# A longer TensorE warm-up in a cached grouped-query attention kernel

## The chip, the cores and the metric

The kernel runs on one core of one Trainium2 chip. Its time is the device time of one execution in microseconds (us); several executions are taken and their median is compared. The five engines of the core have instruction queues of their own and wait for one another by semaphores: TensorE (PE in the profile; its weight loads are shown apart as PEld), VectorE (DVE), ScalarE (ACT), GpSimd (POOL) and SyncE (SP), which here issues every DMA. SBUF is the on-chip working memory, PSUM the small memory of eight banks into which TensorE writes.

## The reference

Two independent problems, A and B, of the same shape are computed and joined along the last axis. Each is a block of attention with a cache of keys and values: 16 batches of 80 rows of 576 numbers, 32 query heads, 16 heads of keys and values (two query heads share one), 512 cached positions, heads of 128.

```python
B, Sq, D = 16, 80, 576
Hq, Hkv, Sk, Dh = 32, 16, 512, 128
...
q = (lambda x, *d: x.transpose(*d))((x @ wq).reshape(B, Sq, Hq, Dh), 0, 2, 1, 3)
k = jnp.repeat(k_cache, rep, axis=1)
v = jnp.repeat(v_cache, rep, axis=1)
scores = jnp.einsum("bhqd,bhkd->bhqk", q, k) * (Dh ** -0.5)
p = _softmax(scores, axis=-1)
o = jnp.einsum("bhqk,bhkd->bhqd", p, v)
return (lambda x, *d: x.transpose(*d))(o, 0, 2, 1, 3).reshape(B, Sq, Hq * Dh) @ wo
```

## The kernel before

**Units.** The work is cut into 128 units, each one batch and four of the 16 key-value heads, so eight query heads. Eight units that share the four heads are an octet with its own slice of wq; four octets are a half problem (eight batches, 640 rows); there are four half problems. A unit has five steps of 128 query rows against 512 positions: step 0 collects the last 32 rows of each of the four heads (four column tiles of TensorE side by side, line 431), steps 1 to 4 take the first 128 rows of a head each (line 436).

**A step.** TensorE computes scores into PSUM bank 0, 1 or 2 (line 431 or 436). VectorE takes the negated maximum of each row (441), ScalarE the exponential with the row's sum (445), VectorE the reciprocals for the five steps of a unit (449), GpSimd scales the rows (452). Eight steps after its scores, TensorE transposes the step's probabilities against the identity matrix (458), VectorE copies them out of PSUM (464, 466), TensorE multiplies by V (501), and ScalarE copies the output into oT (513).

**Around it.** The projections of the next octet (335, evicted by 342 and 347) and the output projections (546, evicted by 560 and 566) are laid between the steps. Keys come by a transposing DMA into one of five buffers (405), values into one of four (409); wq slices alternate between two buffers (288, 292, 295).

**Order.** A small scheduler written into the kernel gives every operation a due time by hand. Operations are sorted by it; each engine runs its own in that order; what an operation reads and writes is named, and from these names the scheduler makes semaphore waits between different engines. TensorE's operations among themselves need no waits. All loads stand in SP's one queue in order of due time, so a load that waits for its buffer holds up the loads behind it.

**The start.** POOL fills `ones` (201), makes `ident`, the 128x128 identity (204), and zeroes part of wq_sb (208). VectorE fills `warm` with zeros (215). TensorE's first operation is the warm-up, `em_warm`: NWARM = 8 matmuls of `ones` against `warm`, 512 columns wide, into PSUM bank 0 (220), which nobody reads. It waits for `ones` and `warm`. Behind it in TensorE's queue stand, in this order:

- the transpositions of the first x block by block, 5 blocks of 5 (line 259, `em_xtr`), into banks 7, 5, 6, 3, 4, each block copied out by VectorE (263, `em_xev`);
- the first projections, for the first two batches: 8 groups of 5 matmuls 160 columns wide (335, `em_qp`), into banks 3, 4, 7, 5, 6 in turn, copied out by ScalarE and VectorE in turn;
- the scores of the first unit (431) and, between them, the rest of the first octet's projections, 480 columns wide.

SP's queue begins with the load of x (248), six loads of wq (288, 295, 292, twice), three loads of K (405), and then V (409) and K in turn.

Of the kernel before, what the change touches and what calls it, by code (L numbers as in the profile page):

```python
# [7 lines left out]
F32 = mybir.dt.float32  # L8
# [126 lines left out]
def bass_concat_heads__gqa_block_cached__gqa_block_cached__near_ridge_kernel(  # L135
# [10 lines left out]
    _, G, SK, DH = A_k_cache.shape  # L146
# [13 lines left out]
    with ExitStack() as es:  # L160
        block = es.enter_context(nc.Block())
        sb = lambda name, shape, dt: es.enter_context(nc.sbuf_tensor(name, shape, dt))
        ident = sb("ident", [128, 128], BF16)
        ones = sb("ones", [128, 128], BF16)
        warm = sb("warm", [128, 512], BF16)
        xs = sb("xs", [128, NRT, D], BF16)
        xT = sb("xT", [128, 2, 5, NROW], BF16)
        wq_sb = sb("wq_sb", [128, 2, 5, 1024], BF16)
# [13 lines left out]
        ps = es.enter_context(nc.psum_tensor("ps", [128, 8, 512], F32))  # L182
        psb = ps[:].bitcast(BF16)
# [5 lines left out]
        S = _Sched()  # L189
# [7 lines left out]
        def R(res, ver):  # L197
            return (res, ver)
# [18 lines left out]
        def em_warm(e):  # L217
            last = None
            for _ in range(NWARM):
                last = e.matmul(ps[:, 0, :], lhsT=ones[:], rhs=warm[:], start=True, stop=True)  # L220
            return last

        if NWARM:
            S.add("dve", -1000, em_warmset, writes=[R(("warm",), 0)], name="warmset")
            S.add("pe", -990, em_warm, reads=[R(("ones",), 0), R(("warm",), 0)], writes=[R(("ps", 0), ("W",))],
                  name="warm")
        IDENT = R(("ident",), 0)

        def su_time(goct, bl):
# [4 lines left out]
        for ph in range(NPH):  # L234
# [11 lines left out]
            def em_ldx(e, x_ap=x_ap, half=half):  # L246
# [4 lines left out]
                  name="ldx%d" % ph)  # L251
            for blk in range(NRT):
# [9 lines left out]
                def em_xev(e, blk=blk, xsl=xsl, xb=xb):  # L262
# [5 lines left out]
                      name="xtr%d.%d" % (ph, blk))  # L268
                S.add("dve", tbase[blk] + KO["xev"], em_xev, reads=[R(("ps", xb), pv_)],
                      writes=[R(("xT", xsl, blk), ph)], name="xev%d.%d" % (ph, blk))  # L270

        QB = ((0, 6), (6, 2))
        for goct in range(NPH * NOCT):
# [20 lines left out]
            def em_ldwb(e, wq_ap=wq_ap, q=q, wsl=wsl):  # L294
# [3 lines left out]
                  name="ldwa%d" % goct)  # L298
            S.add("sp", t_ld + 0.01, em_ldwb, writes=[R(("wq", wsl, "b"), goct)], dsem="d_wq%d" % wsl,
                  name="ldwb%d" % goct)  # L300
# [3 lines left out]
            for i in range(8):  # L304
                for c in range(2):
# [40 lines left out]
                    def em_qev_dve(e, qsl=qsl, b0=b0, nb=nb, n0=n0, n1=n1, col=col, bank=bank):  # L346
# [6 lines left out]
                          reads=[R(("wq", wsl, "a"), goct), R(("wq", wsl, "a2"), goct), R(("wq", wsl, "b"), goct),  # L353
                                 R(("wqz",), 0)]
                          + [R(("xT", xsl, b_), ph) for b_ in blks],
                          writes=[R(("ps", bank), pv_)], name="qp%d.%d.%d" % (goct, i, c))
                    S.add(ev_eng, t + t_ev, em_qev_act if ev_eng == "act" else em_qev_dve,
                          reads=[R(("ps", bank), pv_)],
                          writes=[R(("qT", qsl, bl, i), goct) for bl in range(b0, b0 + nb)],
                          name="qev%d.%d.%d" % (goct, i, c))  # L360
# [31 lines left out]
        for U in range(NSU):  # L392
# [5 lines left out]
            _, kc_ap, vc_ap, _, _ = probs[prob]  # L398
# [8 lines left out]
            def em_ldv(e, vc_ap=vc_ap, b=b, q=q, vs=vs):  # L407
# [4 lines left out]
                  name="ldk%d" % U)  # L412
            S.add("sp", t_v - 5.0 * (NV - 1) + KO["ldv"], em_ldv, writes=[R(("V", vs), U)], dsem="d_v%d" % vs,
                  name="ldv%d" % U)

            for k in range(5):
# [55 lines left out]
                else:  # L472
# [3 lines left out]
                      writes=[R(("ps", sbk), ("S", T))], name="qk%d" % T)  # L476
                S.add("dve", tq + KO["max"], em_max, reads=[R(("ps", sbk), ("S", T))],
                      writes=[R(("nm", si), T)], name="max%d" % T)
                t4 = time_of(5 * G + 4)
                S.add("act", tq + KO["exp"], em_exp, reads=[R(("ps", sbk), ("S", T)), R(("nm", si), T)],  # L480
                      writes=[R(("P", psl), ("e", T)), R(("rs", ss, col), G)], name="exp%d" % T)
                if col == 4:
                    S.add("dve", t4 - LA + KO["rcp"], em_rcp, reads=[R(("rs", ss, k_), G) for k_ in range(5)],
                          writes=[R(("ri", ss), G)], name="rcp%d" % G)
                S.add("pool", t4 - LA + KO["nrm"] + 0.01 * col, em_nrm,
                      reads=[R(("ri", ss), G), R(("P", psl), ("e", T))],
                      writes=[R(("P", psl), ("n", T))], name="nrm%d" % T)
                S.add("pe", t0, em_tr, reads=[R(("P", psl), ("n", T)), IDENT],
                      writes=[R(("ps", tb), ("T", T))], name="tr%d" % T)
                S.add("dve", t0 + KO["ptev"], em_ptev, reads=[R(("ps", tb), ("T", T))], writes=pt_writes,  # L490
                      name="ptev%d" % T)

                if k >= 1:
# [4 lines left out]
                    def em_pv(e, gl=gl, ob=ob, off=off, vs=vs, pts=pts):  # L498
                        last = None
                        for j in range(4):  # L500
# [6 lines left out]
                          reads=[R(("V", vs), U), R(("pT", pts, gl, "A"), U), R(("pT", pts, gl, "R"), U)],  # L507
                          writes=[R(("ps", ob), ("O", U, pr))], name="pv%d.%d" % (U, gl))
                    if gl % 2 == 1:
                        hb = 8 * q + 4 * pr  # L510

                        def em_oev(e, ob=ob, hb=hb, bl=bl):
# [4 lines left out]
                              writes=[R(("oT", bl, q, pr), ph)], name="oev%d.%d" % (U, pr))  # L517

        NB_ = NRT * NOC
        for ph in range(NPH):  # L520
            prob, half = divmod(ph, NPP)
            for hh in range(2):
                for n in range(NB_):
                    r, c3 = divmod(n, NOC)
# [29 lines left out]
                    else:  # L554
                        ot_reads = [R(("oT", b_, 0, hh), ph) for b_ in bls]
                    S.add("pe", t, em_op, reads=ot_reads + [R(("wo", hh, wc_), prob) for wc_ in range(NWC)],
                          writes=[R(("ps", bank), pv_)], name="op%d.%d.%d" % (ph, hh, n))
                    if hh == 0:
                        def em_ea(e, r=r, c3=c3, bank=bank):
# [3 lines left out]
                              writes=[R(("acc", r, c3), ph)], name="oea%d.%d" % (ph, n))  # L563
                    else:
# [4 lines left out]
                        def em_st(e, r=r, c3=c3, prob=prob, half=half, slot=slot):  # L569
# [6 lines left out]
                              writes=[R(("osb", slot), (ph, n))], name="oeb%d.%d" % (ph, n))  # L576
# [73 lines left out]
```

## Time and profile before

| | us |
|---|---|
| median of 3 runs | 818.07 |
| lowest and highest | 814.95, 818.31 |
| span of the profiled execution | 812.5 |
| TensorE busy in it | 797.9 |
| VectorE, ScalarE, GpSimd busy | 680.2, 643.4, 433.0 |
| warm-up matmuls (line 220), start to end | 1.34 to 4.91 |
| first transposition of x (line 259) | 5.63 |
| first projection (line 335) | 9.02 |
| first scores (line 431) | 14.99 |

The time of a run and the span of the profiled execution are two measurements: the span goes from the first instruction of the program to the last, the time also holds what lies around it. In the timeline a row is a group of like instructions: its start, its length, the engine, the line of the kernel, the operation, the tile written and the tiles read, the shape and the count; in brackets the engine's idle time ahead of it and what ended that. Matmuls overlap in the array, so that the length of one (0.2 to 0.6 us) says little of the pace; the pace is the distance from one start to the next. A row of waits is the waiting group, what it waited for, then the total in us, the times and the longest.

### The profile page before, as it was taken

Reading aid. Unit: us, or ns where it says so; the run is one execution under the profiler, and the core shown is the slowest. Engines: PE = TensorE matmul, PEld = TensorE weight load, DVE = VectorE, ACT = ScalarE, POOL = GpSimd, SP = SyncE. Lnnn points to the kernel's source line nnn. Section 1 sums busy time; section 2 is a strip of 40 time slices with the busy share of each in tenths; the row PEclk is TensorE's granted clock in tenths of the full one; section 3 lists DMA queues with packets and bytes.
Section 4 is the critical chain, followed back from the end, with each engine's and each line's share of the span. In section 5 each row is a group of like instructions: output and inputs, shape, how many; then the busy total and the mean of one; then the engine's idle time right before and its main releaser. Section 6 shows DMA issues by size and latency. Waiting matters only on the chain.

```text
span 812.5 us, 23206 instructions
## 1 busy us (share of the span) xinstructions
PE 797.9 (98%) x8940; PEld 620.6 (76%) x8940; DVE 680.2 (84%) x1617; ACT 643.4 (79%) x1725; POOL 433.0 (53%) x647
## 2 busy tenths in 40 slices
PE   7999999999999999999999999999999999999998
PEld 4677678777777777877777777777777778777778
DVE  3899988888888889888888889888888888988872
ACT  2899888888878778888887887888887788888860
POOL 1466665455555546555555555555465455555650
DMA  9999999999897999979789999999978879977601
GB/s 228 243 245 283 249 235 268 260 254 219 190 214 182 224 231 214 207 162 223 180 199 240 245 219 230 237 259 223 224 200 191 200 195 214 199 187 172 156 29 37
DMA packets 363629, 169.94 MB, mean 209 GB/s; under 512 B 278017, under 2 KB 354305, under 8 KB 363521
## 3 DMA queue, kind: packets, MB, share of 16 engines
q1 hardware_dynamic: 363520, 168.46, 90.9%
q8 instruction: 73, 1.20, 0.6%
q14 instruction: 36, 0.29, 0.1%
HBM read 98.37 MB, written 2.95 MB: 125 GB/s over the span
## 4 chain that ended last, share of the span: by engine, by line
PE 90%; DVE 5%; DMA 3%; SPq 0%; issue 0%; POOL 0%; ACT 0%; POOLq 0%
PE ps L335 20%; PE ps L546 19%; PE ps L458 18%; PE ps L501 16%; PE ps L436 12%; PE ps L431 5%; DVE negmax L441 3%; DVE pT L466 1%; DMA kT<-in_A_k_cache_dram 1%; DMA v_sb<-in_A_v_cache_dram 1%; DMA wq_sb<-in_A_wq_dram 1%; PE ps L259 1%; POOL p_sb L452 0%; SPq L292 0%; DVE rinv L449 0%
## 5 line engine op out<-in xcount | busy, mean ns | idle before, releaser
L452 POOL TENSOR_SCALAR p_sb<-p_sb,rinv 128x512 bf16<-128x512 bf16 x640 | 430.5, 695 | 354.6 <-DVE rinv L449 354.6
L445 ACT ACTIVATE p_sb<-ps,negmax 128x512 bf16<-128x512 f32 x640 | 442.3, 691 | 83.4 <-DVE negmax L441 65.3
L441 DVE TENSOR_REDUCE negmax<-ps 128x1 f32<-128x512 f32 x640 | 434.4, 679 | 4.5 <-PE ps L436 2.9
L466 DVE COPY pT<-ps 128x512 bf16<-128x512 bf16 x512 | 209.3, 409 | 93.3 <-PE ps L458 92.6
L458 PE MATMUL ps<-ident,p_sb 128*128 128x128 bf16 x2560 | 248.5, 220 | 4.6 <-DVE negmax L441 3.5
L501 PE MATMUL ps<-pT,v_sb 128*128 128x160 bf16 x2048 | 225.3, 233 | 2.6 <-DMA v_sb<-in_A_v_cache_dram 1.3
L458 PEld LDWEIGHTS ps<-ident,p_sb 128*128 128x128 bf16 x2560 | 175.4, 98 | 57.2 <-DVE qT L347 21.6
L501 PEld LDWEIGHTS ps<-pT,v_sb 128*128 128x128 bf16 x2048 | 169.0, 98 | 63.9 <-DVE qT L347 3.6
L335 PE MATMUL ps<-xT,wq_sb 128*128 128x480 bf16 (+1 forms) x1280 | 214.4, 300 | 1.6 <-DMA wq_sb<-in_A_wq_dram 0.9
L436 PE MATMUL ps<-kT,qT 128*128 128x512 bf16 x512 | 194.0, 379 | 0.0
L546 PE MATMUL ps<-wo_sb,oT 128*128 128x192 bf16 x1920 | 175.7, 246 | 0.0
L546 PEld LDWEIGHTS ps<-wo_sb,oT 128*128 128x128 bf16 x1920 | 158.6, 98 | 0.0
L335 PEld LDWEIGHTS ps<-xT,wq_sb 128*128 128x128 bf16 x1280 | 107.0, 98 | 45.0 <-DVE qT L347 0.9
L513 ACT CAST oT<-ps 128x320 bf16<-128x320 f32 x256 | 108.9, 425 | 35.2 <-PE ps L501 32.9
L445 ACT ACTIVATION_READ_ACCUMULATOR p_sb<-ps,negmax 128x1 f32 x640 | 128.1, 200 | 0.0
L342 ACT ACTIVATE qT<-ps 128x480 bf16<-128x480 f32 (+1 forms) x128 | 71.8, 561 | 25.6 <-PE ps L335 25.5
L464 DVE COPY pT<-ps 128x512 bf16<-128x512 bf16 x128 | 52.9, 413 | 1.3 <-PE ps L458 1.3
L431 PE MATMUL ps<-kT,qT 128*32 128x512 bf16 x512 | 51.2, 390 | 1.4 <-DMA kT<-in_A_k_cache_dram 1.4
L436 PEld LDWEIGHTS ps<-kT,qT 128*128 128x128 bf16 x512 | 50.1, 98 | 0.7
L347 DVE TENSOR_SCALAR qT<-ps 128x160 bf16<-128x160 f32 (+1 forms) x128 | 41.5, 324 | 3.8 <-PE ps L335 3.7
L566 DVE TENSOR_TENSOR osb<-ps,acc 128x192 bf16<-128x192 f32 x60 | 21.0, 349 | 15.3 <-PE ps L546 12.2
L431 PEld LDWEIGHTS ps<-kT,qT 128*32 128x32 bf16 x512 | 13.1, 92 | 14.9 <-DMA kT<-in_A_k_cache_dram 1.6
(16 smaller groups left out, 77.5 us busy)
## 6 DMA issues: line engine op xcount, KB each, us to landing
v_sb<-in_A_v_cache_dram SPq DMA_DIRECT2D x64, 512.0 KB, 4.5
v_sb<-in_B_v_cache_dram SPq DMA_DIRECT2D x64, 512.0 KB, 4.5
wq_sb<-in_A_wq_dram SPq DMA_DIRECT2D x16, 512.0 KB, 5.5
wq_sb<-in_B_wq_dram SPq DMA_DIRECT2D x16, 512.0 KB, 5.5
wo_sb<-in_A_wo_dram SPq DMA_DIRECT2D x8, 576.0 KB, 5.4
wo_sb<-in_B_wo_dram SPq DMA_DIRECT2D x8, 576.0 KB, 4.8
out_dram<-osb SPq DMA_DIRECT2D x60, 48.0 KB, 2.1
xs<-in_A_x_dram SPq DMA_DIRECT2D x2, 720.0 KB, 5.1
```

What stands on the lines that cost most here:

```text
L335: last = e.matmul(ps[:, bank, 0:n1 - n0], lhsT=wq_sb[:, wsl, ck, i * 128:(i + 1) * 128], rhs=xT[:, xsl, ck, n0:n1], start=(ck == 0), stop= ...
L342: return e.activation(qT[:, qsl, b0:b0 + nb, col:col + 80], ps[:, bank, 0:n1 - n0].rearrange("p (b s) -> p b s", b=nb), AF.Identity, scale ...
L431: last = e.matmul(ps[32 * g4:32 * g4 + 32, sbk, :], lhsT=qT[:, qsl, bl, g4 * 160 + 128:g4 * 160 + 160], rhs=kT[:, ks, :, g4 * 128:(g4 + 1) ...
L436: last = e.matmul(ps[:, sbk, :], lhsT=qT[:, qsl, bl, gl * 160:gl * 160 + 128], rhs=kT[:, ks, :, gl * 128:(gl + 1) * 128], start=True, stop ...
L441: return e.tensor_reduce(negmax[:, si:si + 1], ps[:, sbk, :], axis=AX.X, op=AluOpType.max, negate=True)
L445: return e.activation(p_sb[:, psl, :], ps[:, sbk, :], AF.Exp, bias=negmax[:, si:si + 1], scale=1.0, accum_out=rowsum[:, ss, col:col + 1])
L452: return e.tensor_scalar(p_sb[:, psl, :], p_sb[:, psl, :], rinv[:, ss, col:col + 1], 1.0, op0=AluOpType.mult, op1=AluOpType.mult)
L458: last = e.transpose(psb[:, tb, j * 128:(j + 1) * 128], p_sb[:, psl, j * 128:(j + 1) * 128], ident[:])
L466: return e.tensor_copy(pT[:, pts, gl, :, 0:128], psb[:, tb, 0:512].rearrange("p (j n) -> p j n", j=4))
L501: last = e.matmul(ps[:, ob, off:off + 160], lhsT=v_sb[:, vs, gl, j * 128:(j + 1) * 128], rhs=pT[:, pts, gl, j, :], start=(j == 0), stop=(j ...
L513: return e.copy(oT[:, hb:hb + 4, bl * SQ:(bl + 1) * SQ], ps[:, ob, 0:320].rearrange("p (h s) -> p h s", h=4))
L546: last = e.matmul(ps[:, bank, 0:DC], lhsT=oT[:, h, r * 128:(r + 1) * 128], rhs=wo_sb[:, h, c3 * DC:(c3 + 1) * DC], start=(hi == 0), stop=( ...
```

## The change

`em_warm` goes on behind its eight matmuls with 160 more, none of whose results is read: transpositions of the identity in two 64-row and four 32-row tiles of TensorE's array, matmuls of 480 columns in two row tiles, matmuls of 512 columns in four column tiles, matmuls of 32, 64 and 96 columns over the whole array, groups of four matmuls of 256 columns between these, and at the end 16 transpositions of a 32-bit float copy of the identity (4 of the whole, 12 in 64-row tiles). They write PSUM banks 0 to 5. VectorE gets one more operation, the copy of `ident` into the new tile `identf`, behind its fill of `warm`. The warm-up's waits grow by `ident` and `identf`, and stand ahead of its first matmul, as the warm-up is one operation of the scheduler.

```diff
@@ -163,6 +163,8 @@
         ident = sb("ident", [128, 128], BF16)
         ones = sb("ones", [128, 128], BF16)
         warm = sb("warm", [128, 512], BF16)
+        identf = sb("identf", [128, 128], F32)
+        identw = identf
         xs = sb("xs", [128, NRT, D], BF16)
         xT = sb("xT", [128, 2, 5, NROW], BF16)
         wq_sb = sb("wq_sb", [128, 2, 5, 1024], BF16)
@@ -218,12 +220,48 @@
             last = None
             for _ in range(NWARM):
                 last = e.matmul(ps[:, 0, :], lhsT=ones[:], rhs=warm[:], start=True, stop=True)
+            for blk in range(12):
+                for h in range(2):
+                    r = slice(64 * h, 64 * h + 64)
+                    e.transpose(psb[:, 1 + h, blk * 64:blk * 64 + 64], ident[r, :], ident[r, r])
+            for _ in range(4):
+                e.matmul(ps[:, 0, 0:256], lhsT=ones[:], rhs=warm[:, 0:256], start=True, stop=True)
+            for blk in range(12):
+                for h in range(4):
+                    r = slice(32 * h, 32 * h + 32)
+                    e.transpose(psb[:, 1 + h, blk * 32:blk * 32 + 32], ident[r, :], ident[r, r])
+            for _ in range(4):
+                e.matmul(ps[:, 0, 0:256], lhsT=ones[:], rhs=warm[:, 0:256], start=True, stop=True)
+            for _ in range(4):
+                for h in range(2):
+                    r = slice(64 * h, 64 * h + 64)
+                    e.matmul(ps[:, 1 + h, 0:480], lhsT=ones[r, :], rhs=warm[r, 0:480], start=True, stop=True)
+            for _ in range(4):
+                e.matmul(ps[:, 0, 0:256], lhsT=ones[:], rhs=warm[:, 0:256], start=True, stop=True)
+            for _ in range(4):
+                for h in range(4):
+                    e.matmul(ps[32 * h:32 * h + 32, 1, :], lhsT=ones[:, 0:32], rhs=warm[:, :], start=True,
+                             stop=True, tile_position=(0, 32 * h))
+            for n_ in (32, 64, 96):
+                for _ in range(12):
+                    e.matmul(ps[:, 2, 0:n_], lhsT=ones[:], rhs=warm[:, 0:n_], start=True, stop=True)
+            for blk in range(4):
+                e.transpose(ps[:, 3, 0:128], identw[:], identw[:])
+            for blk in range(6):
+                for h in range(2):
+                    r = slice(64 * h, 64 * h + 64)
+                    last = e.transpose(ps[:, 4 + h, blk * 64:blk * 64 + 64], identw[r, :], identw[r, r])
             return last
 
         if NWARM:
             S.add("dve", -1000, em_warmset, writes=[R(("warm",), 0)], name="warmset")
-            S.add("pe", -990, em_warm, reads=[R(("ones",), 0), R(("warm",), 0)], writes=[R(("ps", 0), ("W",))],
-                  name="warm")
+            def em_identf(e):
+                return e.tensor_copy(identf[:], ident[:])
+
+            S.add("dve", -995, em_identf, reads=[R(("ident",), 0)], writes=[R(("identf",), 0)], name="identf")
+            S.add("pe", -990, em_warm,
+                  reads=[R(("ones",), 0), R(("warm",), 0), R(("ident",), 0), R(("identf",), 0)],
+                  writes=[R(("ps", b_), ("W",)) for b_ in range(6)], name="warm")
         IDENT = R(("ident",), 0)
 
         def su_time(goct, bl):
```

## The prediction

> **What bounds the kernel now.** First the page: one engine fills the span, and the chain that ended last runs on it.
>
> ```profile
> span 812.5 us, 23206 instructions
> PE 797.9 (98%) x8940; PEld 620.6 (76%) x8940; DVE 680.2 (84%) x1617; ACT 643.4 (79%) x1725; POOL 433.0 (53%) x647
> PE 90%; DVE 5%; DMA 3%; SPq 0%; issue 0%; POOL 0%; ACT 0%; POOLq 0%
> ```
>
> TensorE is 98% busy, so whatever is put into its queue ahead of real work is paid in full unless it lies in one of the few holes. The holes stand in the second view, TensorE's timeline of the first 17 us (start, length, instructions, in brackets the idle time before and what ended it).
>
> ```profile
> 1.34 3.57 PE L220 MATMUL ps<-warm,ones 128*128 128x512 bf16 x8 [1.34 <-DVE warm L215]
> 5.63 2.85 PE L259 MATMUL ps<-ident,xs 128*128 128x128 bf16 x25 [0.72 <-DMA xs<-in_A_x_dram]
> 9.02 3.25 PE L335 MATMUL ps<-xT,wq_sb 128*128 128x160 bf16 x40 [0.54 <-DVE xT L263]
> 13.04 0.51 PE L335 MATMUL ps<-xT,wq_sb 128*128 128x160 bf16 x5 [0.77 <-DMA wq_sb<-in_A_wq_dram]
> 14.99 0.40 PE L431 MATMUL ps<-kT,qT 128*32 128x512 bf16 x4 [1.44 <-DMA kT<-in_A_k_cache_dram]
> ```
>
> The warm-up ends at 4.9, just before x lands (5.63). The last hole closes at 14.99 with the first K load; behind it come projections and scores without a break. So 14.99, the first L431, is the mark I follow: whatever delays it delays all behind it.
>
> The third view, TensorE's waits over the whole span, tells what a delay could win back:
>
> ```profile
> PE ps L458 <- DVE negmax L441: 3.5, 8, 0.4
> PE ps L431 <- DMA kT<-in_A_k_cache_dram: 1.4, 1, 1.4
> PE ps L501 <- DMA v_sb<-in_A_v_cache_dram: 1.3, 1, 1.3
> PE ps L501 <- DVE pT L466: 1.2, 1, 1.2
> PE ps L335 <- DMA wq_sb<-in_A_wq_dram: 0.9, 2, 0.8
> ```
>
> Behind 15 us, start-to-start gaps above their usual add up to 1.5 us at 94.3 (V late), 1.4 at 110.4 (the pT row; the V load issued at 105.78 behind that of the next x is the likely late one) and 0.3 at 58.2 (wq): 3.2 us that loads may explain. The others lie at the end (741 to 788 us) and have nothing to do with the start.
>
> **The change, part by part.** *Removed:* nothing. *Added on VectorE:* one 128x128 copy into identf, for which TensorE's whole warm-up now waits. It waits for ident, which POOL ends at 1.37. The nearest rows are the memset of warm (0.27 us) and the 128x640 copy (0.49); I take 0.27: start about 1.44, end 1.71, and with the 0.14 us from warmset's end to the first matmul (1.20 to 1.34) the warm-up starts at 1.85 instead of 1.34 (bounds 1.65 to 2.05). Behind that wait stands all of TensorE's queue. The eight old matmuls then take 8 x 0.427 = 3.41 (starts 0.427 apart in the trace): 5.26. No DMA is added and SP's queue isn't touched.
>
> *Added on TensorE:* 160 matmuls, each with its weight load. Prices are start-to-start times, since durations overlap (a 128x128 transposition lasts 0.22 but four lie 0.056 apart). At full clock the trace has 0.056 at 128 columns, 0.069 at 160, 0.083 at 192, 0.2025 at 480, 0.2157 at 512: 0.416 ns a column and 2.6 ns on top, the line through 160 and 512, which makes 0.109 of 256 columns. Column tiles are in the trace:
>
> ```profile
> 33.94 0.39 PE L458 MATMUL ps<-ident,p_sb 128*128 128x128 bf16 x4
> 34.25 0.40 PE L431 MATMUL ps<-kT,qT 128*32 128x512 bf16 x4
> 34.59 0.40 PE L458 MATMUL ps<-ident,p_sb 128*128 128x128 bf16 x4
> 34.82 0.38 PE L436 MATMUL ps<-kT,qT 128*128 128x512 bf16 x1
> ```
>
> The four column tiles start within 0.011 us of each other: tiles run side by side. But going in costs 0.093 extra (0.149 from the last transposition's start, not 0.056) and coming out 0.107 (0.323, not 0.216). Row tiles, moving operands under 128 columns and fp32 aren't in the trace; they are bounded by neighbours. In us:
>
> - 24 transpositions in two 64-row tiles: 0.028 each if pairs overlap, 0.056 if not; middle 0.042: 1.0 (0.7 to 1.3).
> - 48 in four 32-row tiles: 0.014 to 0.056, middle 0.035: 1.7 (0.7 to 2.7).
> - 12 matmuls of 256 columns: 1.3.
> - 8 of 480 columns in two row tiles: 0.8 overlapped, 1.6 one by one; 1.2.
> - 16 column-tile matmuls, four rounds: 0.216 (no change of tiling between rounds) to 0.416 each; 1.0 (0.9 to 1.7).
> - 36 of 32, 64 and 96 columns: 0.416 ns a column gives 1.0, the 128-column row 2.0; 1.5.
> - 16 fp32 transpositions: 0.056 as bf16 up to 0.427, the dearest spacing in the trace; I take 0.318, a weight load and a matmul one behind the other (0.098 + 0.220), as fp32 is twice the bytes and nothing says that its load overlaps: 5.1 (0.9 to 6.8). The least certain term.
> - Ten changes of tiling at 0.1: 1.0 (0.4 to 2.0).
>
> Sum 13.8 (6.6 to 19.4). [...]
>
> *Clock.* The granted clock reads 1.00 throughout, yet the starts show two speeds: L220 at 0.427 for 512 columns and L259 at 0.107 for 128 are half speed, L335 goes from 0.133 to 0.069 at 9.71 us. So the clock rose 8.4 us after the first matmul, across two holes. With no hole it should rise earlier: between right after the eighth matmul (cost 0) and 9.71 (half of the 4.5 us from 5.26 lost: 2.2). I take 1.1. [...]
>
> The warm-up ends at 5.26 + 13.8 + 1.1 = 20.2 (11.7 to 27.1).
>
> *What is late next.* x has landed long before, so L259 starts at 20.2. Its 25 at full clock take 1.4 instead of 2.7; VectorE's five copies out of PSUM then set the pace (0.533 apart in the trace, first 0.5 after the start). The first projection reuses the bank of the fourth copy, free after about 2.6, the second that of the fifth, so the row of projections counts from 2.8; 40 x 0.069 = 2.8, and the last copy out (0.2 + 0.33) lets L431 start 6.1 us after L259. Before it was 14.99 - 5.63 = 9.4: the clock and the gone waits for wq (0.8) and K (1.4) give 3.3 back. So L431 starts at 26.3: 11.3 us late.
>
> *Won back behind it.* SP's queue issues without a hole from 0.8 to 96 us; it runs late on its own account, not because buffers are full:
>
> ```profile
> 36.05 0.58 SPq L409 DMA_DIRECT2D v_sb<-in_A_v_cache_dram  x1
> ...
> 87.64 0.51 SPq L409 DMA_DIRECT2D v_sb<-in_A_v_cache_dram  x1
> 88.19 7.43 SPq L405 DMA_TRANSPOSE kT<-in_A_k_cache_dram  x1
> ```
>
> The V load at 36.05 reuses a buffer that TensorE freed at about 33.75, 2.3 us earlier. With TensorE 11.3 later that load waits for the buffer, SP stands 9 us, and from there on loads are ahead by those 2.3 relative to TensorE, no more, however long the warm-up. That removes the wait at 94.3 and part of 110.4: 2.0 (bounds 0 to 3.2).
>
> Sum: 11.3 - 2.0 = +9.3 us of span, 812.5 to 821.8. The median shown is 5.6 above the profiled span; I carry that: **827.4**.
>
> **Rivals.** *The block is short:* row tiles overlap wholly and fp32 goes in one pass. For the block B and the clock's loss c the net is B + c - 5.6 (5.26 - 8.9 - 2.0, where 8.9 is 14.99 - 6.1). Within 4.1 us (0.5%, about what a measurement of this kernel tells from no change) it stays if B + c is under 9.7; at 8.0 the time is 812.5 + 2.4 + 5.6 = 820.5. For it: tiles 3 to 4 ns apart in L431. Against it: four kinds of instruction must all lie near their lower bound. This is the case on the other side: not slower. *The clock stays down:* small work doesn't raise it, the block runs at half speed, 13.8 becomes 27.6, net 27.6 - 5.6 = +22 and 1.6 more for L259 and L335 as now: 842. Against it: the rise at 9.71 came after 2.5 us of transpositions and few matmuls. *Faster:* the block hides in the hole before x. There are only 5.63 - 5.26 = 0.4 us; 160 instructions would have to take 2 ns each. Even without any the gain is about 2 us of clock and 2.0 won back. *Unread work is dropped:* the eight old matmuls, as unread, all stand in the trace.
>
> **Numbers.** Forecast 0.73, short block 0.14, clock down or a block at its upper bounds 0.11, faster 0.02. Slower 0.84, same 0.14, faster 0.02. The range, 821 to 834, is B + c from 8.5 to 21.5; below lies half of the short block, above the half-clock case.
>
> **What would show it.** TensorE's timeline: L259 starts near 20 with idle 0; its 25 take about 1.6; no DMA releaser before L431, which starts near 26. VectorE gains one copy before 2 us. The fp32 rows near 0.32 apart. The V wait at 94 (then near 105) is gone, and the period from 130 us on is unchanged. I am wrong if L431 starts before 21, if the rows of the block lie 14 ns apart, or if the time behind 15 us moves by more than 3 us against L431.

## The result and the profile after

| | before | after |
|---|---|---|
| median of 13 runs each (us) | 816.15 | 820.21 |
| lowest and highest | 814.95, 818.45 | 817.32, 823.58 |
| span of the profiled execution | 812.5 | 818.1 |
| first transposition of x | 5.63 | 14.27 |
| first scores | 14.99 | 20.36 |
| span from the first scores to the end | 797.47 | 797.77 |

The ratio is 1.0043 with a 95% interval of 1.0027 to 1.0059: 4.06 us slower by the medians, a loss that is clear of the noise and about half a per cent. Two later sets of the changed kernel gave 1.0046 [1.0026, 1.0067] and 1.006 [1.0042, 1.0079]. The forecast was 827.4, 9.3 above the 818.07 it started from, and its range began at 821: right in sign, more than twice too large.

The page of the changed kernel, in the lines shown of before: span, busy time of the engines, and the shares of the chain of work that ended last.

```profile
span 818.1 us, 23525 instructions
PE 803.8 (98%) x9100; PEld 623.9 (76%) x9100; DVE 682.0 (83%) x1618; ACT 643.4 (79%) x1725; POOL 434.1 (53%) x647
PE 93%; DVE 5%; DMA 1%; POOL 0%; issue 0%; ACT 0%; POOLq 0%
```

TensorE has 160 matmuls more and 5.9 us more busy time, close to the 5.6 us of span. The share of DMA in the chain falls from 3% to 1%: the holes of the start are filled with warm-up.

The timeline of the changed kernel's start (start, length, engine, line, and in brackets the idle time ahead and what ended it):

```profile
1.31 1.80 POOL L210 MEMSET wq_sb<- 64x2048 bf16 x1
1.40 1.79 DVE L259 CAST identf<-ident 128x128 f32<-128x128 bf16 x1 [0.21 <-POOL ident L206]
3.24 3.59 PE L222 MATMUL ps<-warm,ones 128*128 128x512 bf16 x8 [3.24 <-DVE identf L259]
6.77 0.82 PE L226 MATMUL ps<-ident 64*128 64x64 bf16 x24
...
13.20 0.62 PE L249 MATMUL ps<-identf 128*128 128x128 f32 x4
13.75 0.59 PE L253 MATMUL ps<-identf 64*128 64x64 f32 x12
14.27 1.57 PE L297 MATMUL ps<-ident,xs 128*128 128x128 bf16 x25
16.50 2.99 PE L373 MATMUL ps<-xT,wq_sb 128*128 128x160 bf16 x40 [0.66 <-DVE xT L301]
19.91 0.52 PE L373 MATMUL ps<-xT,wq_sb 128*128 128x160 bf16 x5 [0.42 <-DVE qT L385]
20.36 0.40 PE L469 MATMUL ps<-kT,qT 128*32 128x512 bf16 x4
```

The warm-up starts at 3.24 and not at 1.85: the cast into identf takes 1.79 us and ends just behind GpSimd's memset of wq_sb (3.11). The same memset stood there before, while VectorE had nothing to do behind its own:

```profile
0.93 0.27 DVE L215 MEMSET warm<- 128x256 uint32 x1 [0.93 <-PEq L635]
1.08 0.29 POOL L204 TENSOR_SCALAR_AFFINE_SELECT ident<-ones 128x128 bf16<-128x128 bf16 x1
1.32 1.80 POOL L208 MEMSET wq_sb<- 64x2048 bf16 x1
```

In the changed kernel the block lies between 6.77 and 14.27. From there the sum goes as forecast: the first scores come 6.09 us behind, and no load is waited for on the way.

TensorE's waits in the changed kernel (in total, times, longest):

```profile
PE ps L496 <- DVE negmax L479: 3.5, 8, 0.4
PE ps L222 <- DVE identf L259: 3.2, 1, 3.2
PE ps L539 <- DMA v_sb<-in_A_v_cache_dram: 2.0, 1, 2.0
PE ps L539 <- DVE rinv L487: 0.9, 1, 0.9
```

The waits for the first K load (1.4) and for wq (0.9) are gone, as forecast. The wait for V, which was to go, grew from 1.3 to 2.0. It now stands at 101.9:

```profile
99.57 0.38 PE L474 MATMUL ps<-kT,qT 128*128 128x512 bf16 x1
101.91 0.44 PE L539 MATMUL ps<-pT,v_sb 128*128 128x160 bf16 x4 [1.96 <-DMA v_sb<-in_A_v_cache_dram]
```

Further on hardly anything differs: TensorE's multiplications by V run 5.61 us behind those of before at 138 us and 5.66 at 773. The stretch from 130 to 160 us (busy time of TensorE, its weight loads, VectorE, ScalarE and GpSimd, granted clock, DMA share, GB/s), first of before:

```profile
130.00:160.00 30.00, 30.00 (x344) 23.50 (x342) 25.65 (x62) 24.76 (x67) 15.95 (x24) 1.00 1.08 269
```

and of the changed kernel:

```profile
130.00:160.00 30.00, 30.00 (x344) 23.63 (x341) 25.74 (x61) 24.85 (x67) 16.57 (x25) 1.00 1.07 261
```

344 matmuls in both. So the difference is made in the first 20 us, and what comes back or is lost later lies between 20 and 130 us.

### The profile page after: what moved, and what is told of

It is laid out like the page before. It is cut to its first block, busy times and chain, and to the rows that moved or that the text cites. A ratio compares the mean times of both kernels' runs of the same rounds, so it can differ in the third digit from the quotient of the medians.

```text
span 818.1 us, 23525 instructions
## 1 busy us (share of the span) xinstructions
PE 803.8 (98%) x9100; PEld 623.9 (76%) x9100; DVE 682.0 (83%) x1618; ACT 643.4 (79%) x1725; POOL 434.1 (53%) x647
## 4 chain that ended last, share of the span: by engine, by line
PE 93%; DVE 5%; DMA 1%; POOL 0%; issue 0%; ACT 0%; POOLq 0%
PE ps L373 21%; PE ps L584 19%; PE ps L496 18%; PE ps L539 16%; PE ps L474 12%; PE ps L469 5%; DVE negmax L479 3%; DVE pT L504 1%; DMA v_sb<-in_A_v_cache_dram 1%; PE ps L297 1%; PE ps L222 0%; POOL p_sb L490 0%; DVE identf L259 0%; DVE xT L301 0%; PE ps L247 0%
## 5 line engine op out<-in xcount | busy, mean ns | idle before, releaser
L487 DVE RECIPROCAL rinv<-rowsum 128x5 f32<-128x5 f32 x128 | 23.1, 180 | 0.5 <-ACT p_sb L483 0.5
```

## The experiments

Ratios are to runs of the kernel before on the same chip, 11 to 35 of them. "The mark" is the start of the first scores (line 431 of before), "the tail" the span from there to the end.

**How firm is the start of before?** The kernel before, unchanged, with a profile of its own.

> The kernel before once more, for the spread of its own runs and of its loads. Theory 1 (the clock's rise differs from run to run and with it the time): the granted clock over the span reads below 1.000 in the slower of these runs as it does in the slower runs of the changed kernel (there 1.000 goes with spans of 815.6 to 818.1, 0.998 with 818.5 to 819.9, 0.996 with 821.2 to 821.8). Theory 2 (only the small matmuls of the added block make the clock fall): it reads 1.000 in all of them. Loads: if the rate of SP's queue differs by itself between executions, the seven V loads from the 7th to the 14th take something other than the 42.2 us of the first profile; the changed kernel took 46.0. First scores (L431) at 15.0 +- 0.3, as the first K load sets it.

Measured: 1.0001 [0.9988, 1.0013]; mark 16.22, tail 798.45. The mark of before isn't fixed: the first K load landed anywhere from 14.89 to 18.26 us over the fifteen profiles of this document that load in this order (the middle one at 16.14), and the profile that the forecast was built on, at 14.95, had the second earliest. In this run TensorE ran at half speed from 8.9 to 15.7 (a granted clock of 0.52 from 9 to 16), and all ten runs show a mean clock below 1.000, as theory 1 allows and theory 2 does not.

**What does the wait for identf cost?** The warm-up as three operations, each with its own waits, so that the eight old matmuls need only `ones` and `warm`, the bf16 part of the block (`em_warm2`) `ident` as well, and only the fp32 part (`em_warm3`) `identf`:

```diff
+            return last
+
+        def em_warm2(e):
...
+            return last
+
+        def em_warm3(e):
...
-            S.add("pe", -990, em_warm,
-                  reads=[R(("ones",), 0), R(("warm",), 0), R(("ident",), 0), R(("identf",), 0)],
-                  writes=[R(("ps", b_), ("W",)) for b_ in range(6)], name="warm")
+            S.add("pe", -990, em_warm, reads=[R(("ones",), 0), R(("warm",), 0)], writes=[R(("ps", 0), ("W",))],
+                  name="warm")
+            S.add("pe", -989, em_warm2, reads=[R(("ones",), 0), R(("warm",), 0), R(("ident",), 0)],
+                  writes=[R(("ps", b_), ("W",)) for b_ in range(6)], name="warm2")
+            S.add("pe", -988, em_warm3, reads=[R(("identf",), 0)],
+                  writes=[R(("ps", b_), ("W",)) for b_ in range(6)], name="warm3")
```

> The changed kernel with its warm-up cut into three operations of the scheduler, so that only the fp32 transpositions wait for identf; the first matmul starts at 1.34 again instead of 3.24. Theory A (the first scores come 6.1 us behind the end of the warm-up, and the rest of the kernel follows them one to one): the warm-up ends at 12.4 (+- 0.5, by when the clock rises) instead of 14.27, L431 starts at 18.5 instead of 20.36, and the time is 1.9 us under the changed kernel's, 2.2 above the kernel before. Theory B (late loads at 94 to 118 us decide the total and swallow small shifts of the start): the time stays within 0.7 us of the changed kernel's.

Measured: 1.0012 [0.9995, 1.0029]. The warm-up starts at 1.33 and ends at 11.56, 2.7 us earlier: 1.9 from the wait, 0.8 from the clock, which here is up about when the block begins (its first 24 transpositions take 0.50 us, against 0.75 in the changed kernel). The first scores could have come at 17.65 (11.56 + 6.09), but K landed at 18.0 in this run. The time is 0.5 above the kernel before (817.12 against 816.59), less than the 2.2 that theory A had added up.

**Why is the cast slow?** GpSimd's memset is put behind the cast; nothing else is touched.

```diff
-        S.add("pool", -998, em_wqz, writes=[R(("wqz",), 0)], name="wqz")
+        S.add("pool", -994, em_wqz, reads=[R(("identf",), 0)], writes=[R(("wqz",), 0)], name="wqz")
```

> The changed kernel with POOL's zeroing of wq_sb (1.8 us) made to wait for identf, so that it no longer runs beside VectorE's copy of ident into identf. Theory A (the copy took 1.79 us instead of the 0.27 forecast because VectorE and GpSimd ran side by side): the copy takes 0.15 to 0.35 us, the warm-up starts at 1.8 instead of 3.24, L297 at 12.8 instead of 14.27, L469 at 18.9, time 1.4 us under the changed kernel's. Rival (a copy from bf16 to fp32 is that slow by itself): 1.79 stays, nothing else moves.

Measured: 1.0004 [0.9989, 1.0019]. Timeline of this kernel's start:

```profile
1.40 0.23 DVE L259 CAST identf<-ident 128x128 f32<-128x128 bf16 x1 [0.21 <-POOL ident L206]
1.68 1.80 POOL L210 MEMSET wq_sb<- 64x2048 bf16 x1 [0.32 <-DVE identf L259]
1.68 3.56 PE L222 MATMUL ps<-warm,ones 128*128 128x512 bf16 x8 [1.68 <-DVE identf L259]
5.18 0.52 PE L226 MATMUL ps<-ident 64*128 64x64 bf16 x24
5.63 0.61 PE L228 MATMUL ps<-warm,ones 128*128 128x256 bf16 x4
6.18 0.52 PE L232 MATMUL ps<-ident 32*128 32x32 bf16 x48
6.63 0.61 PE L234 MATMUL ps<-warm,ones 128*128 128x256 bf16 x4
7.17 0.98 PE L238 MATMUL ps<-warm,ones 64*128 64x480 bf16 x8
8.09 0.61 PE L240 MATMUL ps<-warm,ones 128*128 128x256 bf16 x4
8.63 1.05 PE L243 MATMUL ps<-warm,ones 128*32 128x512 bf16 x16
9.61 1.33 PE L247 MATMUL ps<-warm,ones 128*128 128x32 bf16 x36
10.78 0.62 PE L249 MATMUL ps<-identf 128*128 128x128 f32 x4
11.33 0.59 PE L253 MATMUL ps<-identf 64*128 64x64 f32 x12
11.85 1.57 PE L297 MATMUL ps<-ident,xs 128*128 128x128 bf16 x25
18.31 0.40 PE L469 MATMUL ps<-kT,qT 128*32 128x512 bf16 x4 [0.29 <-DMA kT<-in_A_k_cache_dram]
```

The same cast takes 0.23 us alone and 1.79 beside the memset: that is shown. The rows also price the whole block at full clock, from one start to the next; the table further down uses them. With the warm-up ending at 11.85 the loss can't be told from nothing.

**Which part of the block costs?** First the block without identf and the 16 fp32 transpositions, with the old matmuls free to start (144 bf16 instructions added):

```diff
-            for blk in range(4):
-                e.transpose(ps[:, 3, 0:128], identw[:], identw[:])
...
-            S.add("dve", -995, em_identf, reads=[R(("ident",), 0)], writes=[R(("identf",), 0)], name="identf")
...
+            S.add("pe", -990, em_warm, reads=[R(("ones",), 0), R(("warm",), 0)], writes=[R(("ps", 0), ("W",))],
+                  name="warm")
+            S.add("pe", -989, em_warm2, reads=[R(("ones",), 0), R(("warm",), 0), R(("ident",), 0)],
+                  writes=[R(("ps", b_), ("W",)) for b_ in range(6)], name="warm2")
```

> The changed kernel without identf and without the 16 fp32 transpositions: 144 added matmuls, the warm-up starting at 1.4. It ends at 10.5 as in the split kernel, so TensorE is ready for L431 at 16.6, about when the first K load lands (15.0 to 18.0 in the profiles so far). Theory A: the time is within 1 us of the kernel before and about 1 us under the split kernel's. Rival (every us of the block is paid from 5.6 on): 4.9 above before. Clock: if a warm-up without holes keeps the clock up, most runs read 1.000, as 8 of 12 of the split kernel and only 7 of 45 of the kernel before.

Measured: 815.51, 0.9994 [0.9982, 1.0006].

```profile
10.43 1.56 PE L290 MATMUL ps<-ident,xs 128*128 128x128 bf16 x25
16.51 0.40 PE L462 MATMUL ps<-kT,qT 128*32 128x512 bf16 x4
```

144 added matmuls cost nothing that can be measured: they end at 10.43, and the scores 6.08 us later, at 16.51, come within 0.4 us of the middle landing of K. It beats the changed kernel, but isn't distinguishable from the one before.

Then only the first four groups, 80 instructions, without identf:

```diff
             for _ in range(4):
-                e.matmul(ps[:, 0, 0:256], lhsT=ones[:], rhs=warm[:, 0:256], start=True, stop=True)
+                last = e.matmul(ps[:, 0, 0:256], lhsT=ones[:], rhs=warm[:, 0:256], start=True, stop=True)
             return last
```

> The changed kernel without identf and with only the first four groups of the block (24 and 48 row-tile transpositions, 8 matmuls of 256 columns); the warm-up ends at about 7.3 instead of 4.9 (before) or 14.3. Theory A with its break-even (the end of the warm-up costs nothing until 8.9, as L431 waits for the first K load until 14.99 anyway): L259 starts at 7.3 instead of 5.63, L431 still at 15.0, time within 0.8 us of the kernel before. Rival (every us of warm-up behind 5.6 is paid, since TensorE is 98% busy): L431 at 16.7, time 1.7 above before.

Measured: 1.0005 [0.9992, 1.0017].

```profile
7.59 1.56 PE L271 MATMUL ps<-ident,xs 128*128 128x128 bf16 x25
...
14.74 0.51 PE L347 MATMUL ps<-xT,wq_sb 128*128 128x160 bf16 x5 [1.94 <-DMA wq_sb<-in_A_wq_dram]
17.01 0.62 PE L443 MATMUL ps<-kT,qT 128*32 128x512 bf16 x4 [1.76 <-DMA kT<-in_A_k_cache_dram]
```

The warm-up ends 6.7 us earlier than in the changed kernel, but the scores come only 3.4 earlier, at 17.01 and not at the 15.0 expected: they wait for wq and K instead.

**Is it the kind of instruction or the time?** The block replaced by 30 plain 512-column matmuls, with the wait for identf kept; run twice.

```diff
+            for _ in range(30):
+                last = e.matmul(ps[:, 0, :], lhsT=ones[:], rhs=warm[:], start=True, stop=True)
```

> The changed kernel with 30 matmuls of 512 columns in place of the 160 small ones, same waits, about the same length (warm-up from 3.24 to about 14.3). Theory A: L431 at 20.4 +- 0.6, time as the changed kernel, 4.1 above before. Clock theory 2 (small work in row tiles, column tiles and words lets the clock fall back in some runs): the granted clock reads 1.000 in all runs, the spread shrinks from 6.3 us to that of the kernel before (3.5), and the median is some 1.5 us under the changed kernel's at the same first score. Clock theory 1 (any kernel has these runs): the same mixture of 1.000, 0.998 and 0.996.

> The kernel with 30 dense matmuls in place of the 160 once more, beside the changed kernel on the same chip. Both bring the first scores at 20.4. Theory A (only the moment of the first scores counts): its time is within 0.8 us of the changed kernel's, the earlier gap of 1.5 was chance; V loads 7th to 15th 51 to 53 us. Rival (the small matmuls do something to the loads or the clock behind the start): again 1.5 us or more below the changed kernel, loads at about 51.6 against 52.7 and 54.4.

Measured: 1.003 [1.0014, 1.0046] and 1.0043 [1.0028, 1.0058]. From the first of them:

```profile
6.63 7.83 PE L224 MATMUL ps<-warm,ones 128*128 128x512 bf16 x30
14.30 1.56 PE L268 MATMUL ps<-ident,xs 128*128 128x128 bf16 x25
20.39 0.40 PE L440 MATMUL ps<-kT,qT 128*32 128x512 bf16 x4
```

The same end, the same mark (20.39 against 20.36) and a loss of like size: most of it follows from when the warm-up ends, whatever it is made of. Perhaps not all. On the chip where both ran side by side the dense kernel lies 2.5 us below the changed one (819.07 against 821.58, given further down), with loads of 51.7 us against 54.6; that is what the rival of the second expectation had asked for, though with six runs each, spread over 3 to 4 us, the difference in time isn't firm. The section on the tail comes back to it. The same plain matmuls with no identf, on the kernel before:

```diff
-NWARM = 8
+NWARM = 28
```

> The kernel before with one number changed: 28 old matmuls of 512 columns instead of 8, no small ones, no new wait. The warm-up has no hole and ends at 9.1 (12 at 0.427 until the clock rises near 6, then 0.216 each). Theory A (a warm-up that ends by 9 to 10 costs nothing, as TensorE is then ready for L431 at 15.2 while the first K load landed at 15.0 to 18.3): time not above the kernel before. Clock: without holes most runs read 1.000 as with the bf16 block (10 of 11; the kernel before 8 of 72), and the time lies 0.5 to 1.2 us below the kernel before. Rival (the bf16 block's 815.5 was chance, the warm-up's length is paid): 3.5 above before.

Measured: 1.0007 [0.999, 1.0025]; warm-up 1.33 to 9.62, mark 15.71.

**One to one beyond the cover?** The block twice, `for _rep in range(2):` around it.

> The changed kernel with its block of 160 done twice. The second time it runs at full speed all through, 6.7 us as in the split kernel. Theory A (the rest follows the first scores one to one, nothing is won back): L469 at 27.1, time 6.7 us above the changed kernel's (+-1 for the V holes). Rival, the term of the prediction (loads get ahead and win back what TensorE loses to late V loads, some 3 us): the V holes near 105 and 125 us vanish and the time is 4 above the changed kernel's.

Measured: 826.84, 1.0134 [1.0109, 1.0159].

```profile
20.21 1.57 PE L298 MATMUL ps<-ident,xs 128*128 128x128 bf16 x25
26.30 0.40 PE L470 MATMUL ps<-kT,qT 128*32 128x512 bf16 x4
```

The mark is 5.94 later than with one block. The time is 10.2 above the kernel before on the same chip, 6.1 more than the 4.06 of one block, though from four runs only: beyond the cover (the time in which TensorE would wait for its loads anyway) each us costs about a us, and the 3 us of the rival aren't won back (a hole of 1.89 us remains at 105.8). It also lands where the forecast had put the changed kernel itself (20.2, 26.3, 827.4). Up to the first scores this supports the forecast's way from the warm-up's end onward. That the time agrees as well is luck: from the mark the forecast counted 795.5 us to the end of the span and 5.6 from there to the median, and measured were 798.4 and 2.1. The two blocks take 13.76 us, 13.37 without a hole of 0.39 in the second: about twice the 6.72 of the split kernel. Here the clock was up from the block's start at 6.45 (the first 24 transpositions take 0.46 us against 0.75).

**Do the loads bound the start?** The kernel before, with the first K load ahead of the second octet's wq, and its projections due later:

```diff
+            if goct == 1:
+                x_ld = -22.0
...
+                        if goct == 1 and i == 0:
+                            x += 2.1 if c == 0 else 3.5
```

> The kernel before (no added block) with the second octet's three loads of wq put behind the first K load in SP's queue, and the first two groups of that octet's projections moved behind the first scores. Theory A (the start of the kernel before is bound by the landing of the first K load, at 15 to 18 us, not by TensorE): L431 starts at about 12.5, when the projections are done, and the time falls by 2.5 us less what late V loads take back. Rival (the later V loads decide, as all loads share one queue): L431 earlier, V hole at 94 longer by the same, time unchanged.

Measured: 1.001 [0.9998, 1.0021].

```profile
12.04 0.40 PE L435 MATMUL ps<-kT,qT 128*32 128x512 bf16 x4 [0.41 <-DVE qT L351]
...
18.96 0.52 PE L339 MATMUL ps<-xT,wq_sb 128*128 128x160 bf16 x5 [2.73 <-DMA wq_sb<-in_A_wq_dram]
```

The scores come at 12.04, 3 us before the earliest of before, and the time doesn't move: the wq slice that was moved back is now waited for, for 2.73 us, and behind that hole TensorE runs at half speed to about 23.0 (projections of 480 columns 0.40 us apart from 19.89 on, 0.20 before the hole). Not one load but the row of them sets the start.

**Why isn't the tail shorter, and why do sets of the changed kernel differ?** The changed kernel twice more, unaltered.

> The changed kernel once more, for the spread of its loads. Theory A: L469 at 20.4 +- 0.5 whatever the first K load does. Loads: from the 7th V load to the 15th the first profile took 52.7 us, the slowest of ten profiles (50.2 to 52.7); if that is the loads' own spread, it takes about 51.5 here and the holes of TensorE behind late V loads add up to 2 to 2.5 us rather than 3.2; if the added warm-up slows the loads, again 52.5 or more. Clock: half of the runs at 1.000 as before (6 of 13).

> The changed kernel a third time. Theory A: L469 at 20.4; time 3.5 to 4.1 above the kernel before; V loads 7th to 15th between 51 and 53 us, since 52.7 and 54.4 belong to the spread. Rival: 52.5 or more a third time, holes behind late V loads of 3 us and the clock down behind them in the runs that read 0.998.

Measured: 820.48 and 821.58, ratios as above; marks 20.40 and 20.29, but tails 800.07 and 800.28 against 797.77. The second, around the V wait:

```profile
100.25 0.38 PE L474 MATMUL ps<-kT,qT 128*128 128x512 bf16 x1
103.73 0.44 PE L539 MATMUL ps<-pT,v_sb 128*128 128x160 bf16 x4 [3.10 <-DMA v_sb<-in_A_v_cache_dram]
```

and its stretches of 4 us (columns as above; the clock is the third number from the end):

```profile
100.00:104.00 4.00, 0.90 (x13) 0.58 (x10) 2.39 (x7) 1.89 (x7) 2.43 (x5) 1.00 1.13 318
104.00:108.00 4.00, 4.00 (x25) 2.51 (x23) 1.51 (x3) 2.06 (x5) 0.95 (x2) 0.57 1.07 235
108.00:112.00 4.00, 4.00 (x45) 2.80 (x44) 3.81 (x11) 3.08 (x10) 0.99 (x2) 1.00 1.15 251
```

V is late by 3.1 us instead of 2.0, and behind the hole the granted clock falls to half from 104.5 to 107.9: 25 matmuls in a stretch that else holds 45. The longer hole (1.0 and 1.1 us) and the lost clock (half of 3.4 us) come to 2.7 and 2.8; these tails are 2.3 and 2.5 longer. It is no matter of this kernel alone: the repeat of before had a hole of 2.32 at this place, with half speed from 97.7 to 101.1. But it is more frequent: the mean granted clock of the whole run fell short of 1.000 (by 0.002 or more; by estimate at least one such stretch of 3.4 us at half, as 0.002 of 820 us is 1.6) in 14 of 24 runs of the changed kernel and in 5 of 18 of the dense one. In the other runs the two kernels have the same median, 818.7; in these it is 821.7 and 820.9. So with the same mark and the clock up the two cost the same, and some 2 us of the changed kernel's median (820.7 over the 24 runs) are not the mark's but come from this. Before can't serve as a measure here: 99 of its 120 runs beside the experiments fall short too, and in its repeat above two of the three stretches were lost at the start.

The loads went against theory A both times. From the seventh V load's issue to the fifteenth's they took 54.4 and 54.6 us, where their own spread was to give about 51.5 and then 51 to 53. With the 52.7 of the first profile the three profiles of the changed kernel are the three longest of all sixteen; the others, the dense kernel's among them, have 50.2 to 52.0. Chance hardly explains that, so something in the changed kernel is likely to slow these loads. Two kernels were to find what. The block as 160 plain matmuls of 96 columns, as many instructions as the block has:

```diff
+            for _ in range(160):
+                last = e.matmul(ps[:, 0, 0:96], lhsT=ones[:], rhs=warm[:, 0:96], start=True, stop=True)
```

> The changed kernel with 160 plain matmuls of 96 columns over the whole array in place of its 160 (no row or column tiles, no fp32), same waits. It is as many instructions as the changed kernel and about as long: 2.5 us at half speed, then 0.042 each, first scores near 19.7 to 20.5. If the number of TensorE instructions ahead of the start is what slows the later loads: V loads 7th to 15th take 52.5 us or more, one hole of 2 to 3.3 us near 100, time as the changed kernel (some 820.7). If it is the kind (tiles or fp32): 51 to 52 us as with the 30 dense matmuls, time some 818.8.

And the block with only its 16 fp32 transpositions exchanged for 16 plain bf16 matmuls:

```diff
-            for blk in range(4):
-                e.transpose(ps[:, 3, 0:128], identw[:], identw[:])
...
+            for _ in range(16):
+                last = e.matmul(ps[:, 3, 0:160], lhsT=ones[:], rhs=warm[:, 0:160], start=True, stop=True)
```

> The changed kernel with its 16 fp32 transpositions replaced by 16 bf16 matmuls of 160 columns (1.1 us both); identf is still copied and waited for, so the start is the same: first scores at 20.4. If fp32 in TensorE is what slows the later loads: 51 to 52 us for the V loads 7th to 15th and some 818.8. If it is the tiles or the number of instructions: 52.5 or more and some 820.7.

Measured: 819.08, 1.0035 [1.0018, 1.0052], and 820.71, 1.0046 [1.003, 1.0063]; marks 19.84 and 20.30. By the expectations the first median speaks for the kind of instruction and the second against fp32, which would leave the tiles. But the medians turn on how many runs had the clock short of 1.000, 4 of 10 and 6 of 10 (821.2 and 821.1 in these, 818.3 and 818.8 in the others), and four of ten and six of ten are not told apart. The profiled run of each was one with the clock up (holes of 0.8 us near 99, tails 796.49 and 796.21, loads of 51.3 us in both), so neither profile shows the case in question. The fp32 part isn't needed for the clock to fall, as without it six of ten runs fell; whether the tiles or the number of instructions matter isn't shown.

## Why the prediction was wrong

The method held: follow the mark, add what the warm-up adds, take off what comes back. Its terms did not. Of the span, 3.7 too large, the block makes -7.4, the cast +1.4 and the tail +2.3; the distance from span to median adds another -3.9, and 0.3 comes back, as the profiled run (819.88) was that much below the median. The text's own test of being wrong, first scores before 21, was met.

*The block* failed most. The working took 13.8 for it and 1.1 for the clock; it took 7.50 (6.77 to 14.27). By its own terms, against the rows at full clock of the kernel with the late memset (which contain the changes of tiling):

| term | predicted | measured |
|---|---|---|
| 24 transpositions, 64-row tiles | 1.0 | 0.45 |
| 48 transpositions, 32-row tiles | 1.7 | 0.45 |
| 12 of 256 columns | 1.3 | 1.63 |
| 8 of 480 columns, row tiles | 1.2 | 0.92 |
| 16 in column tiles | 1.0 | 0.98 |
| 36 of 32, 64, 96 columns | 1.5 | 1.17 |
| 16 fp32 transpositions | 5.1 | 1.07 |
| ten changes of tiling | 1.0 | in the others |
| clock | 1.1 | 0.83 (7.50 - 6.67) |

The fp32 term alone is 4.0 of the 7.4 us of error. It was put at a load and a matmul one behind the other; the trace has the 128-column fp32 transpositions 0.109 us apart, twice the 0.056 of bf16, and the load hidden (the four loads lie from 13.16 to 13.58, the matmuls from 13.20 to 13.82). The row tiles were put at the middle between side by side and one by one; they run wholly side by side (a pair of 64 rows 0.054 apart at half clock, a four of 32 rows 0.027). Where the trace of before showed the thing itself, the price was right: column tiles 1.0 against 0.98, and a change of tiling at 0.1 against 0.094 to 0.10 in the block (0.295 from the last row-tile pair to the next matmul where 0.20 would do).

*The cast* failed in the other direction: 0.27 predicted, 1.79 measured, the start 1.4 later than put. The price came from a copy that ran alone and a memset that ran beside a GpSimd operation of 0.29 us; this one ran beside GpSimd's memset of 1.80, which the profile of before had at that very place.

*The clock* was right: forecast 1.1 (0 to 2.2), measured 0.83. The starts of the 256-column matmuls went from 0.213 to 0.109 apart at 9.16, 5.9 us after the first matmul. It is a draw, though: in the double block, with the same matmuls in front, the clock was up by 6.45, 3.2 us after the first, and the block lost nothing.

*What is late next* was right to a hundredth: 6.1 behind the warm-up, measured 6.09, 6.09, 6.09, 6.08, 6.09 in five kernels (14.27 to 20.36, 14.30 to 20.39, 20.21 to 26.30, 10.43 to 16.51, 9.62 to 15.71), unless K lands later. Its parts were not: VectorE's copies come 0.40 apart and not 0.533, the first projection 2.23 behind x and not 2.8, and the group of five projections at 19.91, with its wait of 0.42 for a copy out of PSUM, has no term in the working. That these differences cancel is luck.

*Won back, -2.0*, failed for the changed kernel: the tail is 0.3 longer. The first half of the reasoning happened, the V load that was 2.3 us behind its free buffer is issued 0.03 behind it now. But the loads after it did not stay ahead: the stretch from the seventh V load's issue to the fifteenth's took 52.7 us against 50.2, and the V wait grew (1.3 to 2.0) instead of going. With the block twice, another 6 us of lead, it was 51.3. In other kernels with as late a mark about half of the term seems to come back: with the clock up the tails are 796.2 to 796.5 in four profiles (dense twice, 160 plain matmuls, without fp32), against 797.3 to 797.5 where the mark lies at 15.0 to 16.5 (before, the bf16 block, 28 old matmuls). But tails scatter by as much (795.9 and 797.2 at marks of 18.3 and 18.0), so that a gain from the lead isn't shown; the full 2.0 was seen in none of them with a late mark, and in the changed kernel the slow loads outweigh it.

*Plus 5.6 from span to median* failed: profiled time less span is 1.7 to 1.8 in the fifteen profiles for which both are known (814.7 and 816.41, 818.1 and 819.88). The rest was two draws. The median of three runs, 818.07, lies 1.9 above the 816.15 of thirteen; and the profiled execution, with K at 14.95, would by that distance have taken 814.2, 1.9 below it and as little as the quickest of 120 runs of before (814.15). The step took these for a constant. It makes 3.9 us of the error.

The sum now: warm-up's start +1.9 (1.34 to 3.24), old matmuls as before (3.53 to the next start, at half clock), block 7.50, x copies and projections 6.09: mark 20.36, 5.37 later than in the profile of before; tail +0.30; span +5.67, with 812.5 rounded 5.6. Against the middle K landing, 16.14, the mark is 4.2 late and the sum 4.5; the medians differ by 4.06. That agrees better than it should: the later two sets differ by 3.2 and 5.8 from before on their chips, the dense kernel, with the same mark, by 2.2 and 3.3.

So the rival "the block is short" was the true case, with B + c = 7.5 where it had named 8.0 and 820.5; it was given 0.14. Its reason was half right: the row tiles overlap wholly, but fp32 goes at twice the spacing of bf16 (0.109 against 0.056 us) and not, as the rival had it, at the same. And that its 820.5 comes within 0.3 of the median is partly luck, as it has none of the cast's +1.4, the tail's +2.3 and the distance's -3.9, which cancel. The objection to it, that all four kinds would have to lie near the lower bound, was weak: three of them hang on one question, whether work in separate tiles overlaps, which the column tiles in the trace of before had answered, and fp32, at 1.07, lay close to its lower bound of 0.9. The middle of each range was not a cautious choice where one answer moves them all.

What of the change costs is shown for the larger part: the end of the warm-up at 14.27, since plain matmuls that end there lose 2.2 and 3.3 us. Neither of its two late pieces alone would be seen. Without the slow cast (11.85) or with the old matmuls freed from it (11.56) the loss is not measurable, and the 144 bf16 instructions are free. The cover is the x, wq and K loads: first scores can't come before K at 14.9 to 18.3, so a warm-up that ends 6.1 before that, at 8.8 to 12.2, should cost nothing; kernels in which it ends at 9.62 to 11.85 lose nothing that can be measured.

Open is why runs of the changed kernel get the long V hole and the clock's fall so often; that is the rest of the loss. Up to the K load issued at 51.3 to 51.6 us the load queues of the changed and the dense kernel agree to 0.3 us; the next, issued near 58, holds the queue for 5.6 to 6.4 us in the changed kernel's three profiles and 4.8 to 4.9 in the dense kernel's two. What lengthens it wasn't found.

## What to carry to other kernels

Here work put into a start that waits for loads cost nothing that could be measured up to the last load's landing less the work that must follow (warm-ups that end at 9.62 to 11.85), and about one to one beyond (6.1 us of time for 5.94 of mark in the double block): find that point first, from several profiles, since it moved by 3 us from run to run (K at 14.89 to 18.26). Price an added operation from a row where the same neighbours are busy (the cast took 0.23 us alone, 1.79 beside the memset), and ask of all unknown prices whether one assumption stands behind them. Don't carry the distance between one profiled span and a median: compare that profile's own time.

## What was not expected of the hardware

- A cast of 128x128 from bf16 to fp32 on VectorE took 0.23 us alone and 1.79 beside a GpSimd memset, ending 0.08 behind it. The price is nearly the whole memset (1.80); what holds the cast back isn't shown.
- Transpositions in fp32 are 0.109 us apart at 128x128, against 0.056 in bf16; in two 64-row tiles 0.060 for a pair, 3 to 9 ns within it.
- In the warm-up's block, matmuls of 32, 64 and 96 columns, each with a weight load of 128x128, are 0.025, 0.029 and 0.042 us apart at full clock.
- Holes of TensorE of 2.32, 2.93 and 3.10 us in mid-kernel were followed by about 3.4 us at half clock in three profiles (the repeat of before, with a granted clock of 0.62 from 98 to 102 us, and the two repeats of the changed kernel, with 0.60 and 0.57 from 104 to 108). The double block, with a hole of 1.89, has a mean clock of 0.998 over its run, as those two repeats have. Yet behind one of 1.96 (the changed kernel's first profile) the clock read 1.00, and the bf16 block, with one of 1.75, has 1.000 over its run.
